# Second pass of a fused attention and gated feed-forward kernel: queue order of the x low parts, and the pace of the weight conversions

## The chip, the cores and the metric

One core of one Trainium2 chip runs the whole program. The metric is the device time of one execution in microseconds; a kernel's time is the median of its runs.

## The reference

Block-causal attention (8 batches, 8 heads, 576 tokens, head size 64, blocks of 64), followed by a feed-forward layer with a product of two branches:

```python
scores = scale * np.matmul(q, k.transpose(0, 1, 3, 2))
scores = np.where(block_i >= block_j, scores, -1000000000.0)
attn = softmax(scores)
x = (attn @ v).transpose(0, 2, 1, 3).reshape(4608, 512)
out = ((x @ w_a) * (x @ w_b)) @ w_out        # 512 -> 1536 -> 512
```

Everything is fp32 and the weights come to the chip as 64-bit floats.

## The kernel before, in words

**Products in three parts.** TensorE works on fp32r operands here. Each fp32 operand is split into a high part (a copy rounded by ScalarE) and a low part (operand minus high part, made by VectorE or GpSimd), and each product is the sum of three matmuls: high x high, high x low, low x high. So each activation that enters a product first needs a copy on ScalarE (line 110 or lines 680 to 684) and a subtraction (line 113 or lines 687 to 691).

**Stages.** The hidden dimension of 1536 is cut into 12 blocks of 128, numbered f. Up to about 690 us the attention runs together with the first pass of the feed-forward layer over f = 0 to 3 (`first_pass`). Then comes the loop at line 800, with two rounds: `ps_ = 0` works on f = 4 to 7 and `ps_ = 1` on f = 8 to 11. The text calls this loop the second pass. Each round goes over `NT2 = 6` tiles of 768 tokens. In this document tiles are counted through: tiles 0 to 5 are `ps_ = 0`, tiles 6 to 11 are `ps_ = 1`.

**A tile.** It is four units (`pair_unit`, one per f) and then `pair_out`. A unit computes seven products with a fast 2x2 scheme: y, x, w and v first, and then three more products accumulate in the banks of x, w and v. Between them VectorE adds the partial results: `u = x + u` (line 726), `t = w + u` (728), `t = v + t` (730), `c = w + u` (732), `t = c * t` (733), `u = v + u` (735), `u = x * u` (736, remembered as `last["hf"]`). Line 726 reads x's bank, and the next x product is added into that bank, so TensorE waits for line 726. The results t and u are split by ScalarE (line 110) and GpSimd (line 113) into (hb, lb) and (ha, la). `pair_out` multiplies these with the output weights: 96 matmuls on line 754, those of hb ahead of those of ha; line 813 adds the partial sums of earlier rounds, and line 814 stores them. Unit and `pair_out` together are 4 x 42 + 96 = 264 matmuls.

**Next tile's x.** `load_x` (line 660) loads raw x of the next tile on SP's queue. `sums_x` (line 669) forms the seven sums that the fast scheme needs, for two halves kp = 0 and 1: first the sums and the high parts (lines 675 to 684), then the low parts `xl` (lines 687 to 691). The low parts of kp = 0, and the first two of kp = 1, are on VectorE; the last two of kp = 1 (lines 690 and 691) are on GpSimd. `xl` has one buffer per half, so a low part can be written only when the last unit of the tile in work has read the old one. `nm` is the tile's name, `"0_1"` to `"0_6"` for what is prepared during `ps_ = 0`.

**Conversions.** `convert_w` turns 64-bit weights into fp32 high and low parts: per part five VectorE operations (lines 139, 143, 145, 147, 149), one ScalarE operation, and then sums and splits (lines 165 to 178, or line 110 with 113). It is a generator; each `next` issues one step. During `ps_ = 0` the weights of f = 8 to 11 are converted: 8 parts `wab` of six steps and then 4 parts `wo` of five steps, 68 steps in all, on operand buffers with one copy each. Finished parts go through one staging buffer `st` to HBM (`wabd`, `wod`, line 205), and are loaded from there (lines 839 and 854) when tile 5 has freed the weight buffers. `background(start + k * T2 / 2.4 / pace)` at line 827 is called at each matmul of a unit and issues steps until the count is reached; `pace` is `STEP2` from tile 1 on. At line 851, behind `pair_out` of tile 5, `background(1e4)` issues whatever is left.

**What sets the order.** The framework orders each engine's queue at compile time: an instruction that is ready earlier by its own model of time may go ahead of one that stands earlier in the program, and the engine then runs its queue strictly in order. `behind_of(ins, key)` adds an edge that waits for nothing at run time, but puts `ins` behind the instruction `last[key]` in the queue of its engine. Conversion steps have had such an edge to `last["hf"]` all along; so have two of the x sums of `"0_6"` (line 678).

Of the kernel before, what the change touches and what calls it, by code (L numbers as in the profile page):

```python
# [14 lines left out]
ALU = mybir.AluOpType  # L15
# [23 lines left out]
MORE = 6  # L39
PREF = True  # L40
STEP = 800
STEP2 = 1600
LATE = 1
LO2 = lambda nc: nc.vector
CONVP = [1]*12
# [7 lines left out]
def attention_then_bilinear_ffn(  # L53
# [10 lines left out]
    nc = tc.nc  # L64
# [40 lines left out]
    def f32(ap):  # L105
        return ap.bitcast(F32)

    def split(hi, lo, src, hi_eng, lo_eng):
        if hi_eng is nc.scalar:
            nc.scalar.copy(hi, src)  # L110
        else:
            hi_eng.tensor_copy(hi, src)
        return lo_eng.tensor_tensor(lo, src, f32(hi), op=ALU.subtract)  # L113

    last = {}

    def behind_of(ins, key):
        if key in last:
            tc.add_manual_dep(ins.ins, last[key].ins.name, NOSYNC, reason="after work that is waited for")
# [35 lines left out]
    def parts(fs):  # L155
        return [(f, i) for f in fs for i in range(KP)] + [(f, KP) for f in fs]
# [23 lines left out]
    def convert_w(todo, lo_eng, paced=False, stage=None):  # L180

        def ahead(f, i):
            return fetch(wab[f, :, i] if i < KP else wo[f], f"w{f}_{i}")

        raw = ahead(*todo[0])
        for k, (f, i) in enumerate(todo):
            now, raw = raw, ahead(*todo[k + 1]) if k + 1 < len(todo) else None
            xf, spare = yield from convert(now, f"w{f}_{i}", paced)
            if stage:
                st = stage.tile([P, 2, NW if i < KP else NO, P], F32R, tag="st", name=f"st{f}_{i}")  # L190
            if i == KP:
                if not stage and w_sb[f][1] is None:
                    new_wo(f)
                o = st.rearrange("p j c n -> p j (c n)") if stage else w_sb[f][1]
                split(o[:, 0], o[:, 1], xf, nc.scalar, lo_eng)
            elif f < F1:
                ab = w_sb[f][0]
                hi, lo = (ab[:, j, i].rearrange("p c n -> p (c n)") for j in range(2))
                split(hi, lo, xf, nc.scalar, lo_eng)
            else:  # L200
                ab = st if stage else w_sb[f][0][:, i]
                yield from sums(ab[:, 0], ab[:, 1], xf, spare, paced)
            if stage:
                f -= F1 + F2
                nc.sync.dma_start(wod[f] if i == KP else wabd[f, i], f32(st).rearrange("p j c n -> p (j c n)"))
            yield
# [18 lines left out]
    def h_tile(kind, n, dt, nm):  # L225
        return hpool.tile([P, T2], dt, tag=f"h{kind}", name=nm, bufs=(10, 6)[kind])[:, :n]
# [419 lines left out]
    def bank(nm):  # L646
        nonlocal n_bank
        n_bank += 1
        return (ps_mm if n_bank % 8 < 2 else ps_more).tile([P, 512], F32, tag="mm", name=nm)
# [19 lines left out]
    def sums_x(raw, kp, nm):  # L669

        hi = xk.tile([P, NW, T2], F32R, tag="xh", name=f"xh_{nm}_{kp}", bufs=3)
        t = tpool.tile([P, 3, T2], F32, tag="xt", name=f"xt_{nm}_{kp}")
        a, b = raw[2 * kp:2 * kp + 2]
        v = nc.vector
        for ins in (v.tensor_tensor(t[:, 1], b[:, 1], a[:, 1], op=ALU.subtract),
                    v.tensor_tensor(a[:, 1], a[:, 1], a[:, 0], op=ALU.subtract)):
            if nm == f"0_{NT2}":
                behind_of(ins, "hf")
        v.tensor_tensor(t[:, 0], b[:, 1], a[:, 1], op=ALU.subtract)
        nc.scalar.copy(hi[:, 0:2], a)  # L680
        nc.scalar.copy(hi[:, 2:4], t[:, :2])
        v.tensor_tensor(t[:, 2], b[:, 0], t[:, 0], op=ALU.subtract)
        nc.scalar.copy(hi[:, 4:6], b)
        nc.scalar.copy(hi[:, 6], t[:, 2])
        yield
        lo = xk.tile([P, NW, T2], F32R, tag="xl", name=f"xl_{nm}_{kp}", bufs=2)
        v.tensor_tensor(lo[:, 0:2], a, f32(hi[:, 0:2]), op=ALU.subtract)
        v.tensor_tensor(lo[:, 2:4], t[:, :2], f32(hi[:, 2:4]), op=ALU.subtract)
        e = nc.gpsimd if kp else v
        e.tensor_tensor(lo[:, 4:6], b, f32(hi[:, 4:6]), op=ALU.subtract)  # L690
        e.tensor_tensor(lo[:, 6], t[:, 2], f32(hi[:, 6]), op=ALU.subtract)
        yield hi, lo


# [3 lines left out]
    def pair_unit(f, xs, nm, hs, halves):  # L698

        w = w_sb[f][0]  # L700
        y, x, w_, v_ = (bank(f"ps{i}_{nm}")[:, :T2] for i in "yxwv")

        def prod(ps, what, start, kps=range(KP)):
            iw, ix = what
            for kp in kps:
                (xh, xl), wt = xs[kp], w[:, kp]
                for i, j in ((0, xh), (0, xl), (1, xh)):
                    nc.tensor.matmul(  # L708
                        ps, wt[:, i, iw], j[:, ix], start=start and kp == 0 and i == 0 and j is xh,
                        stop=kp == KP - 1 and i == 1, skip_group_check=not start)  # L710
                    yield

        if halves:
            for ps, what, kp in ((y, Y, 0), (x, X1, 0), (w_, W1, 0), (y, Y, 1), (x, X1, 1), (v_, V1, 0),
                                 (w_, W1, 1), (v_, V1, 1)):
                yield from prod(ps, what, True, [kp])
        else:
            for ps, what in ((y, Y), (x, X1), (w_, W1), (v_, V1)):
                yield from prod(ps, what, True)
        k = (f - F1) % F2  # L720
        (ha, la), (hb, lb) = (
            [h_tile(int(4 * k + 2 * j + i >= 10), T2, F32R, f"h{i}_{nm}_{j}") for i in range(2)] for j in range(2))
        u, t, c = (upool.tile([P, T2], F32, tag=f"u{i}", name=f"u{i}_{nm}", bufs=2 - i // 2) for i in range(3))
        v = nc.vector
        nc.scalar.copy(u, y)
        v.tensor_tensor(u, x, u, op=ALU.add)  # L726
        yield from prod(x, X2, False)
        v.tensor_tensor(t, w_, u, op=ALU.add)  # L728
        yield from prod(w_, W2, False)
        v.tensor_tensor(t, v_, t, op=ALU.add)  # L730
        yield from prod(v_, V2, False)
        v.tensor_tensor(c, w_, u, op=ALU.add)
        v.tensor_tensor(t, c, t, op=ALU.mult)  # L733
        split(hb, lb, t, nc.scalar, nc.gpsimd)
        v.tensor_tensor(u, v_, u, op=ALU.add)
        last["hf"] = v.tensor_tensor(u, x, u, op=ALU.mult)
        split(ha, la, u, nc.scalar, nc.gpsimd)
        hs[f] = (ha, la), (hb, lb)

    def pair_out(fs, hs, nm, out):  # L740

        todo = [(j, o) for j in (1, 0) for o in range(NO)]
        n = {}

        def run(j, o, fs_):
            k = j, o
            if k not in n:
                n[k] = 0, bank(f"pso{j}_{o}_{nm}")[:, :T2]
            i, ps = n[k]
            osl = slice(o * P, (o + 1) * P)  # L750
            for f in fs_:
                (hh, hl), wt = hs[f][j], w_sb[f][1]
                for a, b in ((0, hh), (0, hl), (1, hh)):
                    nc.tensor.matmul(ps, wt[:, a, osl], b, start=i == 0, stop=i == 3 * len(fs) - 1)  # L754
                    i += 1
            n[k] = i, ps
            if i == 3 * len(fs):
                out(j, o, ps)

        for k in todo[:2]:  # L760
            run(*k, fs[:-1])
        for k in todo[:2]:
            run(*k, fs[-1:])
        for k in todo[2:]:
            run(*k, fs)
# [14 lines left out]
    k = 0  # L780
# [8 lines left out]
    for kp in range(KP):  # L789
        g = sums_x(raw, kp, "0_0")  # L790
        next(g)
        xs.append(next(g))
# [4 lines left out]
    k = 0  # L797


    for ps_ in range(2):  # L800
        fs = list(range(F1 + ps_ * F2, F1 + (ps_ + 1) * F2))
        for tt in range(NT2):
# [18 lines left out]
            nm = f"z{ps_}_{tt}"  # L821
# [23 lines left out]
            if ps_ == 0 and tt == 0:  # L845
                background(1e4)
                conv = convert_w(parts(range(F1 + F2, NF)), nc.vector, paced=True, stage=stage)
                n_conv, start, k, pace = 0, 0, 0, STEP2
            pair_out(fs, hs, nm, out)
# [44 lines left out]
```

## Time and profile before

| what | value |
|---|---|
| median of 3 runs | 1277.81 us (1276.7 to 1278.86) |
| profiled execution | 1281.83 us |
| its span, first to last instruction | 1279.8 us |
| granted TensorE clock over the span | 0.988 |
| first product of tile 0, of tile 1 | 698.79 us, 747.01 us |
| first product of tile 6, end of the last tile's products | 993.57 us, 1276.28 us |

The profile is of one execution. It lists, for each engine, busy time and idle time with what ended the wait; the windows view gives busy times between two moments, and the timeline each instruction with its start and duration. Matmuls are pipelined, so in a full stream TensorE starts one about every 0.176 us although each lasts 0.34 us.

### The profile page before, as it was taken

The page shows a single profiled execution, that of the slowest core. Times are in us where ns is not written, and L with a number is a line of the kernel's source. Part 1 is how long each engine was busy: PE and PEld are TensorE (multiplying, and loading weights), DVE is VectorE, ACT ScalarE, POOL GpSimd, SP SyncE. Part 2 cuts the span into 40 slices and gives each one's busy share as a digit, 9 for nine tenths or more (in the row PEclk, how much of TensorE's full clock was granted, in tenths as well). Part 3 has the DMA queues.
Part 4 walks back from the last instruction along what each step waited for, and adds up shares of the span by engine and source line. Part 5 has one row for each costly group of instructions (what it writes and reads, how often), then busy time and mean ns, then how long its engine had stood idle before and what let it go on. Part 6 is the DMA issues. An engine that isn't in the chain of part 4 may idle for free.

```text
span 1279.8 us, 23524 instructions
## 1 busy us (share of the span) xinstructions
PE 1239.3 (97%) x7849; PEld 1173.2 (92%) x7849; DVE 999.2 (78%) x2389; ACT 683.6 (53%) x1722; POOL 554.9 (43%) x679
## 2 busy tenths in 40 slices
PE   9988999999999999999988998999999999999998
PEld 5668998999999999999988998999999999999998
DVE  6878887777887877877699999899967577577553
ACT  5788787788787788888745423233222222122210
POOL 4567565566665565665422322223223123123231
PEclk8999999999999999999998999999999999999999
DMA  5467766777767767676225355364466442243131
GB/s 195 132 167 201 187 174 175 178 171 181 170 167 179 179 171 176 167 178 155 87 94 171 100 180 194 139 206 164 141 220 244 145 149 79 70 149 98 52 99 62
DMA packets 93496, 196.58 MB, mean 154 GB/s; under 512 B 11968, under 2 KB 52928, under 8 KB 93376
## 3 DMA queue, kind: packets, MB, share of 16 engines
q1 hardware_dynamic: 88768, 185.64, 51.4%
q10 hardware_dynamic: 4608, 9.44, 2.0%
q8 instruction: 63, 1.03, 0.3%
q14 instruction: 57, 0.47, 0.1%
HBM read 96.47 MB, written 47.19 MB: 112 GB/s over the span
## 4 chain that ended last, share of the span: by engine, by line
PE 71%; DVE 15%; DMA 4%; issue 4%; ACT 3%; POOL 2%; SPq 1%; ACTq 0%; DVEq 0%; POOLq 0%
PE pso_z L754 13%; PE ps L217 12%; PE tp L468 7%; PE psx_z L708 6%; PE psw_z L708 6%; PE psv_z L708 6%; PE pso L217 4%; PE s L392 4%; PE psy_z L708 3%; PE av L517 3%; PE av L523 3%; PE sl L392 2%; DMA kp<-kT 2%; PE av L507 2%; DVE sw L147 1%
## 5 line engine op out<-in xcount | busy, mean ns | idle before, releaser
L113 POOL TENSOR_TENSOR h_z<-u_z,h_z 128x384 fp32r<-128x384 f32 x96 | 112.8, 1175 | 391.4 <-ACT h_z L110 379.8
L217 PE MATMUL ps<-xh,wab 128*128 128x288 f32 x1024 | 241.8, 304 | 1.2 <-ACT a L241 1.2
L754 PE MATMUL pso_z<-h_z,wo 128*128 128x384 f32 x1152 | 204.0, 335 | 4.5 <-POOL h_z L113 4.5
L445 POOL TENSOR_SCALAR e<-e,rc 128x512 f32<-128x512 f32 (+3 forms) x256 | 151.6, 604 | 127.9 <-DVE rc L442 118.1
L754 PEld LDWEIGHTS pso_z<-h_z,wo 128*128 128x128 f32 x1152 | 199.6, 188 | 7.0 <-POOL h_z L113 7.0
L217 PEld LDWEIGHTS ps<-xh,wab 128*128 128x128 f32 x1024 | 172.3, 189 | 4.7 <-ACT a L241 1.4
L472 DVE TENSOR_TENSOR al<-tp,ah 128x512 fp32r<-128x512 f32 x224 | 131.6, 608 | 31.5 <-ACT ah L470 31.0
L217 PE MATMUL ps<-xl,wab 128*128 128x288 f32 x512 | 154.1, 301 | 0.0
L468 PE MATMUL tp<-ident,e 128*128 128x128 f32 x832 | 136.1, 278 | 10.4 <-POOL e L445 4.0
L470 ACT CAST ah<-tp 128x512 fp32r<-128x512 f32 x224 | 116.4, 531 | 50.3 <-PE tp L468 47.5
L110 ACT CAST h_z<-u_z 128x384 fp32r<-128x384 f32 x96 | 49.3, 514 | 167.7 <-DVE u_z L733 160.2
L217 PE MATMUL pso<-hh,wo 128*128 128x288 f32 x512 | 128.1, 311 | 4.3 <-ACT hh L110 4.3
L708 PE MATMUL psx_z<-xh,wab 128*128 128x384 f32 x384 | 118.5, 344 | 7.2 <-DVE u_z L726 6.7
L468 PEld LDWEIGHTS tp<-ident,e 128*128 128x128 f32 x832 | 100.8, 142 | 25.7 <-POOL e L445 9.5
L401 ACT ACTIVATE e<-s,nm 128x192 f32<-128x192 f32 (+2 forms) x192 | 101.5, 529 | 32.4 <-DVE nm L398 23.2
L708 PE MATMUL psw_z<-xh,wab 128*128 128x384 f32 x384 | 117.0, 340 | 0.8 <-DVE u_z L728 0.8
L708 PE MATMUL psv_z<-xh,wab 128*128 128x384 f32 x384 | 116.7, 339 | 0.5 <-DVE u_z L730 0.4
L398 DVE TENSOR_REDUCE nm<-s 128x1 f32<-128x192 f32 (+3 forms) x256 | 109.9, 431 | 2.4
L217 PEld LDWEIGHTS ps<-xl,wab 128*128 128x128 f32 x512 | 96.5, 188 | 3.4
L217 PEld LDWEIGHTS pso<-hh,wo 128*128 128x128 f32 x512 | 88.3, 192 | 6.6 <-ACT hh L110 5.3
L113 POOL TENSOR_TENSOR v<-vr,v 128x320 fp32r<-128x320 f32 x56 | 50.2, 897 | 89.3 <-ACT v L110 67.9
L392 PE MATMUL s<-k,q 128*128 128x256 f32 x336 | 81.2, 322 | 2.2 <-ACT e_s L401 1.9
(142 smaller groups left out, 2919.5 us busy)
## 6 DMA issues: line engine op xcount, KB each, us to landing
k<-kp SPq DMA_DIRECT2D x112, 288.0 KB, 3.8
xr<-xd SPq DMA_DIRECT2D x48, 384.0 KB, 3.5
pt<-part SPq DMA_DIRECT2D x96, 192.0 KB, 3.5
q<-qp SPq DMA_DIRECT2D x112, 160.0 KB, 2.6
raww<-wab SPq DMA_DIRECT2D x24, 512.0 KB, 3.8
qp<-qT SPq DMA_DIRECT2D x32, 320.0 KB, 3.2
vr<-vm SPq DMA_DIRECT2D x64, 160.0 KB, 3.1
kp<-kT SPq DMA_DIRECT2D x32, 288.0 KB, 3.5
```

What stands on the lines that cost most here:

```text
L110: nc.scalar.copy(hi, src)
L113: return lo_eng.tensor_tensor(lo, src, f32(hi), op=ALU.subtract)
L217: mm = nc.tensor.matmul(ps, w_, d_, start=(i == 0), stop=(i == n - 1))
L392: mark = nc.tensor.matmul(ps[:, :w], qm[:, q0[t]:q0[t] + P], kk[:, :w], start=(i == 0), stop=(i == len(ks) - 1))
L398: nc.vector.tensor_reduce(nm[:, t:t + 1], view, axis=AX.X, op=ALU.max, negate=True)
L401: nc.scalar.activation(out, view, AF.Exp, bias=bias, accum_out=sm[:, t, :1])
L445: nc.gpsimd.tensor_scalar(ev, ev, rc[:, t:t + 1], 1.0, op0=ALU.mult, op1=ALU.mult)
L468: mark = nc.tensor.transpose(tp[:, c], src, ident)
L470: nc.scalar.copy(ah[:, :m, cols], tp[:, :m])
L472: return nc.vector.tensor_tensor(al[:, :m, cols], tp[:, :m], f32(ah[:, :m, cols]), op=ALU.subtract)
L708: nc.tensor.matmul(ps, wt[:, i, iw], j[:, ix], start=start and kp == 0 and i == 0 and j is xh, stop=kp == KP - 1 and i == 1, skip_group_ch ...
L754: nc.tensor.matmul(ps, wt[:, a, osl], b, start=i == 0, stop=i == 3 * len(fs) - 1)
```

## The change

Three edits. `STEP2`, the pace of the conversions from tile 1 on, goes from 1600 to 2800. The four low-part subtractions of `sums_x` get an ordering edge for the tiles prepared during `ps_ = 0`, except the very first: those on VectorE behind `last["hf"]` (line 736 of the last unit), and the two GpSimd ones of kp = 1 behind `last["la"]`. `pair_unit` remembers its last GpSimd split as `last["la"]`.

```diff
-STEP2 = 1600
+STEP2 = 2800
...
         lo = xk.tile([P, NW, T2], F32R, tag="xl", name=f"xl_{nm}_{kp}", bufs=2)
-        v.tensor_tensor(lo[:, 0:2], a, f32(hi[:, 0:2]), op=ALU.subtract)
-        v.tensor_tensor(lo[:, 2:4], t[:, :2], f32(hi[:, 2:4]), op=ALU.subtract)
         e = nc.gpsimd if kp else v
-        e.tensor_tensor(lo[:, 4:6], b, f32(hi[:, 4:6]), op=ALU.subtract)
-        e.tensor_tensor(lo[:, 6], t[:, 2], f32(hi[:, 6]), op=ALU.subtract)
+        for k, ins in enumerate((
+                v.tensor_tensor(lo[:, 0:2], a, f32(hi[:, 0:2]), op=ALU.subtract),
+                v.tensor_tensor(lo[:, 2:4], t[:, :2], f32(hi[:, 2:4]), op=ALU.subtract),
+                e.tensor_tensor(lo[:, 4:6], b, f32(hi[:, 4:6]), op=ALU.subtract),
+                e.tensor_tensor(lo[:, 6], t[:, 2], f32(hi[:, 6]), op=ALU.subtract))):
+            if nm[0] == "0" and nm != "0_0":
+                behind_of(ins, "la" if k > 1 and kp else "hf")
         yield hi, lo
...
         last["hf"] = v.tensor_tensor(u, x, u, op=ALU.mult)
-        split(ha, la, u, nc.scalar, nc.gpsimd)
+        last["la"] = split(ha, la, u, nc.scalar, nc.gpsimd)
```

## The prediction

> **What bounds the kernel now.** I read the page first, then the windows view cut at the first product of each tile, the list of what TensorE waited for, and the timelines of VectorE and GpSimd at the places found.
>
> ```profile
> span 1279.8 us, 23524 instructions
> PE 1239.3 (97%) x7849; PEld 1173.2 (92%) x7849; DVE 999.2 (78%) x2389; ACT 683.6 (53%) x1722; POOL 554.9 (43%) x679
> ```
>
> TensorE (PE) is the bound. The change touches only the loop that begins near 699 us, so what matters is how far its tiles are from an undisturbed one. The next answer has tiles 1 to 7, one to a row: length, then busy time of each engine with its count, granted clock, DMA share and GB/s.
>
> ```profile
> core 0: us, PE busy (x) PEld busy (x) DVE busy (x) ACT busy (x) POOL busy (x), PEclk, DMA share, GB/s
> 747.01:799.95 52.94, 47.58 (x265) 45.45 (x265) 48.96 (x86) 17.63 (x30) 13.58 (x10) 1.00 0.53 175
> 799.95:848.53 48.58, 47.34 (x265) 45.57 (x265) 43.69 (x76) 15.55 (x27) 13.52 (x10) 1.00 0.49 158
> 848.53:897.37 48.84, 47.26 (x266) 45.55 (x265) 46.47 (x81) 17.05 (x29) 13.49 (x10) 1.00 0.54 187
> 897.37:945.79 48.42, 47.51 (x266) 45.62 (x265) 41.65 (x64) 13.11 (x23) 13.47 (x10) 1.00 0.47 151
> 945.79:993.57 47.78, 46.73 (x266) 46.19 (x265) 32.19 (x52) 12.36 (x21) 12.49 (x10) 1.00 0.71 249
> 993.57:1043.93 50.36, 48.27 (x266) 47.78 (x265) 34.33 (x56) 12.77 (x23) 13.14 (x10) 0.97 0.44 141
> 1043.93:1090.39 46.46, 46.46 (x265) 46.29 (x265) 31.33 (x51) 11.37 (x20) 13.14 (x10) 1.00 0.34 107
> ```
>
> Tile 7 is the floor: 46.46 us, TensorE busy throughout, VectorE 31.33. Over it, tiles 1 to 5 lose 6.48 + 2.12 + 2.38 + 1.96 + 1.32 = 14.26 us and tile 6 loses 3.90. That is the most that this change can win, apart from a little in tile 0. VectorE explains where: tiles 1 to 4 hold 17.6 + 12.4 + 15.1 + 10.3 = 55.4 us more VectorE time than tile 7, which is the conversions. What TensorE waited for, in tiles 1 to 5, then from 994 us on, then around tile 0:
>
> ```profile
> PE psx_z L708 <- DVE u_z L726: 4.3, 8, 1.5
> PE pso_z L754 <- POOL h_z L113: 4.0, 3, 2.6
> PE psw_z L708 <- DVE u_z L728: 0.8, 2, 0.4
> PE psv_z L708 <- DVE u_z L730: 0.4, 1, 0.4
> ```
>
> ```profile
> PE psx_z L708 <- DVE u_z L726: 2.1, 1, 2.1
> ```
>
> ```profile
> PE pso_z L754 <- POOL h_z L113: 0.6, 1, 0.6
> PE psx_z L708 <- DVE u_z L726: 0.3, 1, 0.3
> ```
>
> Two kinds of wait, then: inside units for VectorE's sums, and at the start of `pair_out` for the last unit's split on GpSimd (POOL). The named waits of tiles 1 to 5 are 9.5 us and the tiles lose 14.26; the rest is slower restarts after each wait and weight loads that waited. So I size the sum by the tiles' lengths and use the waits only to say what belongs to which edit.
>
> **Part 1, the low parts behind the last product.** The end of tile 1, VectorE first, then POOL (start, duration, line):
>
> ```profile
> 779.84 0.55 DVE L732 TENSOR_TENSOR u_z<-psw_z,u_z 128x384 f32<-128x384 f32 x1
> 780.31 0.94 DVE L687 TENSOR_TENSOR xl<-xr,xh 128x768 fp32r<-128x768 f32 x1
> 781.17 0.55 DVE L733 TENSOR_TENSOR u_z<-u_z,u_z 128x384 f32<-128x384 f32 x1
> ...
> 782.11 0.95 DVE L688 TENSOR_TENSOR xl<-xt,xh 128x768 fp32r<-128x768 f32 x1
> 782.98 0.55 DVE L736 TENSOR_TENSOR u_z<-psx_z,u_z 128x384 f32<-128x384 f32 x1
> ...
> 788.48 1.78 DVE L688 TENSOR_TENSOR xl<-xt,xh 128x768 fp32r<-128x768 f32 x1
> ```
>
> ```profile
> 782.57 2.20 POOL L690 TENSOR_TENSOR xl<-xr,xh 128x768 fp32r<-128x768 f32 x1 [6.48 <-ACT xh L683]
> 784.71 1.73 POOL L113 TENSOR_TENSOR h_z<-u_z,h_z 128x384 fp32r<-128x384 f32 x1
> ```
>
> The edges take L687 and L688 out from between L732 and L736: L733 comes 0.87 us earlier (781.17 - 0.87 = 780.30) and L736 1.7 us. L690 on POOL, which stood ahead of the split, goes behind both splits, so the split could start near 782.6 rather than 784.71. Both gains act on the wait of 2.6 us; together they are 2.1 to 3.0, so I take it as gone. The other two waits in the 4.0 are 1.4 us together and go by the same two steps; of tile 0's 0.6 us I count all, since L733's 0.87 covers it. Nothing is added but edges. What is moved later is 4 low parts of kp = 0 and 2 of kp = 1 on VectorE, and 2 on POOL. All VectorE work in this stretch stays the same, so what is behind it (the additions of line 813, the release of raw x and with it four loads on SP) moves by under 2 us. The next tile's products start 17 us after the last unit (96 of the tile's 264 matmuls, 46.46 x 96/264), and VectorE's low parts end at 790.3 now, 11 us after L732 read that unit's products: covered, with 4 us to spare after such a move. If that cover were gone, each us late would be a us on TensorE.
>
> There is a price inside: the low part now meets the split on POOL.
>
> ```profile
> 1068.53 1.02 POOL L113 TENSOR_TENSOR h_z<-u_z,h_z 128x384 fp32r<-128x384 f32 x1 [0.33 <-POOL h_z L113]
> 1075.40 1.46 POOL L113 TENSOR_TENSOR h_z<-u_z,h_z 128x384 fp32r<-128x384 f32 x1 [5.85 <-ACT h_z L110]
> ```
>
> In tile 7 the split takes 1.02 us inside the tile, and 1.46 us at its end, where VectorE runs low parts. A low part in front of it costs at worst its own duration, 0.95 us (L688 above). The Trainium skill, SBUF — State Buffer, "Who interferes with whom", says that a VectorE instruction with two SBUF inputs and a GpSimd one that reads SBUF lock each other out, and that the second to start waits for the whole first. The 0.44 us of tile 7 agree with it; which of the two would start first behind L736 no trace here shows.
>
> **Part 2, the slower conversions.** 8 parts of six steps and 4 of five are 68 steps. A tile issues 4 x 42 = 168 calls at 160/1600 step each, 16.8 steps; at 2800 it is 9.6. So before, the steps end after four tiles; afterwards five tiles take 48 steps, which are exactly the 8 `wab` parts, and the last 20 steps, the 4 `wo` parts, come in one go at line 851. A step costs 55.4 / 68 = 0.82 us of VectorE.
>
> What a step does to TensorE is seen where a unit begins:
>
> ```profile
> 756.93 0.56 DVE L736 TENSOR_TENSOR u_z<-psx_z,u_z 128x384 f32<-128x384 f32 x1
> 757.40 1.01 DVE L139 TENSOR_SCALAR sw<-raww 128x512 int32<-128x512 int32 x1
> 758.34 0.41 DVE L143 TENSOR_SCALAR mw<-raww 128x512 int32<-128x512 int32 x1
> 758.78 1.40 DVE L145 SCALAR_TENSOR_TENSOR mw<-raww,mw 128x512 f32<-128x512 uint16 x1
> 760.10 0.55 DVE L726 TENSOR_TENSOR u_z<-psx_z,u_z 128x384 f32<-128x384 f32 x1
> ```
>
> Three steps, released by L736, are 1.01 + 0.41 + 1.40 = 2.8 us ahead of L726, for which TensorE waits. With fewer steps there are 2 or 3 instead of 4 to a unit (42 x 160/2800 = 2.4). That this brings down the loss more than in proportion I can't count on: 2 or 3 steps still fit into the same spot. So I scale: tiles 2 and 3 have no part-1 wait of size, and lose 2.12 + 2.38 = 4.5 us over 12.4 + 15.1 = 27.5 us of conversions, 0.164 us each. Five tiles with 48 x 0.82 = 39.4 us lose 6.4 us. The bounds: nothing, if two steps always fit, and 5 x 2.25 = 11.3 us, if each tile loses what tiles 2 and 3 lose now. The linear value lies between and is the only one with a row behind it.
>
> **Part 3, the 20 steps at line 851.** They are 20 x 0.82 = 16.4 us of VectorE, queued behind tile 5's last unit: part fills the 17 us of `pair_out`, the rest lies among tile 6's first units. Four `wo` parts in a row have been there before, in tile 0:
>
> ```profile
> 704.71 0.68 DVE L113 TENSOR_TENSOR wo<-xw,wo 128x512 fp32r<-128x512 f32 x1
> 718.92 0.68 DVE L113 TENSOR_TENSOR wo<-xw,wo 128x512 fp32r<-128x512 f32 x1
> ```
>
> (718.92 - 704.71) / 3 = 4.7 us a part, and TensorE waited only 0.3 us for VectorE there (row above). Here each part also passes the single staging buffer and HBM. What tile 6 loses now has another cause:
>
> ```profile
> 997.20 0.56 DVE L675 TENSOR_TENSOR xt<-xr,xr 128x384 f32<-128x384 f32 x1 [2.12 <-DMA xr<-xd]
> 999.46 0.55 DVE L726 TENSOR_TENSOR u_z<-psx_z,u_z 128x384 f32<-128x384 f32 x1
> ```
>
> VectorE stands still for a load of tile 7's x, with tile 6's L726 queued behind it; TensorE waits 2.1 us, and the clock row says 0.97, (1 - 0.97) x 50.36 = 1.5 us more. With 16 us of conversions in the same queue, this wait may be covered, or the loads come later still. At the rate above the burst alone costs 16.4 x 0.164 = 2.7 us. I take tile 6's loss as unchanged at 3.9, made up otherwise. Bounds: 1 us (the wait covered, tile 0's 0.3 and some restarts) and 16 us (rival 1). The `wo` loads of line 854 have until tile 6's `pair_out`, one tile of 46 us after tile 5's.
>
> **Sum.** 14.3 - 6.4 = 7.9 from tiles 1 to 5, 0.6 from tile 0, 0 from tile 6: 8.5 us. The profiled execution goes from 1281.8 to 1273.3. It lies 4.0 us over the median of the runs, so the median goes from 1277.8 to 1269.3.
>
> **Rivals.**
>
> 1. *Slower: the last 20 steps run in series with their DMAs.* Per part a raw load and a store:
>
> ```profile
> raww<-wo SPq DMA_DIRECT2D x12, 512.0 KB, 3.4
> wod<-st SPq DMA_DIRECT2D x4, 512.0 KB, 3.0
> ```
>
> If neither is hidden, a part takes 4.7 + 3.4 + 3.0 = 11.1 us, and four take 44 us, of which `pair_out` covers 17. The other 28 us, 2.5 parts, lie in tile 6, and in each VectorE stands 6.4 us with unit work queued behind: 16 us in place of 3.9. That gives 1269.3 + 12 = 1281. It turns the sign once tile 6 loses over 3.9 + 8.5 + 2.6 = 15 us. Against it: the next raw load is issued one part ahead, and tile 0's four parts hid theirs. For it: the one staging buffer and VectorE's 2.12 us wait for a load at this very place. Chance 0.07.
>
> 2. *The steps that hurt stay.* If each of tiles 1 to 5 goes on losing 2.25 us, 3.0 us are won there and 0.6 in tile 0, and the burst's 2.7 come on top of tile 6: about 0.9 us won, 1276.9. For it: what stands between L736 and L726 is already only three steps. Against it: tile 4 lost less with fewer conversions. Chance 0.12.
>
> 3. *Tile 6 comes free as well.* If the burst covers the load, tile 6 loses 1 us: 1266.4. Chance 0.16.
>
> 4. *The low parts lock out POOL's split.* If L687 starts first at every tile's end, the split is 0.95 us later than I have it in each of the three waits of 4.0 us, which then keep some 2.6 us: 1271.9. This is the case that the skill's rule of the lock makes possible. Chance 0.10.
>
> That the edges do nothing is excluded for L687, L688 and L690, which stand in front of what they are now to follow.
>
> **Numbers.** The forecast, 1269.3, has 0.55. From 1264.5 (rival 3, with tiles 1 to 5 losing 4.5 rather than 6.4) to 1276.0 (rival 2 with a little won in proportion) it holds 8 in 10; what is left out is rival 1 and most of rival 2. The bound of 0.2%, 2.6 us, is about what a measurement tells from no change. Faster: forecast and rivals 3 and 4, 0.81. Within 0.2%: rival 2, 0.12. Slower: rival 1, 0.07.
>
> **What the changed profile would show.** Right: L687 behind L736 at the ends of tiles 0 to 5, the split of the last unit ahead of L690, no wait of `pso_z` for POOL over 0.5 us; tiles 1 to 5 each 47 to 48.5 us with VectorE near 39 busy; `wo` parts from `pair_out` of tile 5 into tile 6's first units. Wrong: a `pso_z` wait that stays, tiles 2 to 4 at 48.5 or more, or tile 6 over 54 us.

## The result and the profile after

The changed kernel takes 1271.91 us (median of 9 runs, 1269.18 to 1276.22) against 1277.81 of before: a ratio of 0.9944, 95% interval 0.9930 to 0.9958. So it won 5.9 us where 8.5 were forecast. Its profiled execution took 1273.54 us, span 1271.6. A second measurement (e14 below) gave 0.9909 (0.9881 to 0.9936): the size of the gain is known to a few us only.

The windows view of the changed kernel, cut like that of before at the first product of each tile (tiles 1 to 7; line numbers of the unit and of what follows are 3 higher than before, and the low parts are lines 689 to 692):

```profile
core 0: us, PE busy (x) PEld busy (x) DVE busy (x) ACT busy (x) POOL busy (x), PEclk, DMA share, GB/s
745.34:792.32 46.98, 46.69 (x266) 45.79 (x266) 41.67 (x68) 13.70 (x26) 13.22 (x10) 1.00 0.44 137
792.32:839.55 47.23, 47.01 (x266) 45.87 (x265) 42.77 (x69) 14.55 (x26) 12.98 (x10) 1.00 0.47 154
839.55:887.10 47.55, 47.22 (x266) 45.98 (x266) 42.98 (x71) 15.53 (x27) 13.26 (x10) 1.00 0.48 158
887.10:934.58 47.48, 47.14 (x265) 45.96 (x265) 40.55 (x65) 12.09 (x22) 13.26 (x10) 1.00 0.44 140
934.58:983.33 48.75, 47.14 (x266) 46.18 (x265) 40.18 (x66) 13.11 (x23) 13.24 (x10) 1.00 0.78 276
983.33:1035.80 52.47, 49.48 (x265) 48.68 (x265) 46.33 (x80) 19.03 (x31) 13.77 (x10) 0.93 0.67 219
1035.80:1082.25 46.45, 46.45 (x266) 46.28 (x265) 31.33 (x51) 11.38 (x20) 13.18 (x10) 1.00 0.34 104
```

Tiles 1 to 5 now lose 0.52 + 0.77 + 1.09 + 1.02 + 2.29 = 5.69 us over the floor of 46.46, instead of 14.26. Tile 6 loses 6.01 instead of 3.90. Tile 0 is as long as before (48.33 and 48.22). That is 6.4 us won in the loop. The span shrank by 8.2; the other 1.8 us lie ahead of the loop, where nothing was changed: tile 0's first product is at 697.02 instead of 698.79. Over the 14 profiles of this study that moment lies between 694.4 and 701.8 us, so it is scatter. The tiles' lengths repeat far better (5.69 and 5.61 us for tiles 1 to 5, 6.01 and 5.53 for tile 6, in two profiles of the changed kernel), and the experiments are read by them first. One thing can spoil this: a stretch of some 3 us in which TensorE's granted clock is halved. It comes after some waits and not after others (last section), and it is most of the reason why tiles 1 to 5 lose 14.26 us in the profile of before and 16.15 in that of e9, whose program is the same up to there.

What TensorE waited for in the changed kernel, in tiles 1 to 5, then from 982 us on, then around tile 0:

```profile
PE psx_z L711 <- DVE u_z L729: 1.7, 4, 1.2
PE pso_z L757 <- POOL h_z L113: 0.4, 1, 0.4
```

```profile
PE psx_z L711 <- DVE u_z L729: 1.7, 1, 1.7
PE psw_z L711 <- DVE u_z L731: 1.3, 1, 1.3
```

```profile
PE pso_z L757 <- POOL h_z L113: 0.8, 1, 0.8
PE psx_z L711 <- DVE u_z L729: 0.2, 1, 0.2
```

The waits of `pair_out` for GpSimd fell from 4.0 to 0.4 us, and those for VectorE from 5.5 to 1.7. The end of tile 1 shows the new order, VectorE and then GpSimd:

```profile
775.42 0.56 DVE L736 TENSOR_TENSOR u_z<-u_z,u_z 128x384 f32<-128x384 f32 x1
775.90 0.55 DVE L738 TENSOR_TENSOR u_z<-psv_z,u_z 128x384 f32<-128x384 f32 x1
776.48 0.56 DVE L739 TENSOR_TENSOR u_z<-psx_z,u_z 128x384 f32<-128x384 f32 x1
776.96 1.62 DVE L689 TENSOR_TENSOR xl<-xr,xh 128x768 fp32r<-128x768 f32 x1
```

```profile
776.73 2.73 POOL L113 TENSOR_TENSOR h_z<-u_z,h_z 128x384 fp32r<-128x384 f32 x2 [5.36 <-PE psv_z L711]
779.43 2.58 POOL L691 TENSOR_TENSOR xl<-xr,xh 128x768 fp32r<-128x768 f32 x1
```

The low part (L689) is behind the last product (L739), and both splits go ahead of the low part on GpSimd. In tile 6 something else shows:

```profile
988.14 0.55 DVE L676 TENSOR_TENSOR xr<-xr 128x384 f32<-128x384 f32 x1
988.61 0.68 DVE L149 TENSOR_TENSOR xw<-mw,sw 128x512 f32<-128x512 f32 x1
989.21 0.55 DVE L729 TENSOR_TENSOR u_z<-psx_z,u_z 128x384 f32<-128x384 f32 x1
991.10 0.43 DVE L139 TENSOR_SCALAR sw<-raww 128x512 int32<-128x512 int32 x1 [1.34 <-DMA raww<-wo]
```

The leftover conversions stand in VectorE's queue around tile 6's first sums: L729 comes late, and behind it L139 of the next `wo` part waits 1.34 us for its raw weights while L731, for which TensorE waits, is queued behind it. The two waits of TensorE in tile 6 are 1.7 + 1.3 = 3.0 us. The granted clock of tile 6, 0.93, stands for (1 - 0.93) x 52.47 = 3.7 us by estimate; together this is more than the 6.0 us that the tile loses, so the two overlap in part.

### The profile page after: what moved, and what is told of

Its sections match the earlier page's. It is cut to its first block, busy times and chain, and to the rows that moved or that the text cites. A ratio compares the mean times of both kernels' runs of the same rounds, so it can differ in the third digit from the quotient of the medians.

```text
span 1271.6 us, 23516 instructions
## 1 busy us (share of the span) xinstructions
PE 1235.8 (97%) x7849; PEld 1172.4 (92%) x7849; DVE 1006.1 (79%) x2389; ACT 683.3 (54%) x1722; POOL 556.9 (44%) x679
## 4 chain that ended last, share of the span: by engine, by line
PE 74%; DVE 14%; issue 3%; DMA 3%; ACT 3%; POOL 2%; SPq 0%; ACTq 0%; DVEq 0%; POOLq 0%
PE pso_z L757 14%; PE ps L217 12%; PE tp L468 7%; PE psx_z L711 7%; PE psw_z L711 6%; PE pso L217 5%; PE psv_z L711 5%; PE s L392 4%; PE av L517 3%; PE psy_z L711 3%; PE av L523 3%; PE sl L392 2%; DMA kp<-kT 2%; DVE sw L147 1%; DVE nm L398 1%
## 5 line engine op out<-in xcount | busy, mean ns | idle before, releaser
L468 PE MATMUL tp<-ident,e 128*128 128x128 f32 x832 | 135.8, 278 | 11.1 <-POOL e L445 4.0
```

The costliest lines, as they stand in the source:

```text
L468: mark = nc.tensor.transpose(tp[:, c], src, ident)
```

## The experiments

My theory at this point: the edges removed the waits for GpSimd, the pace the waits for VectorE, and the 20 steps issued in one go at the end of tile 5 (the burst) are what tile 6 loses. The rivals: the pace does all, or the edges do all, or tile 6 loses by the loads of tile 7's x as it did before. The table has, for each, what tiles 1 to 5 and tile 6 lose over 46.46 us a tile in its profile, and the ratio to the kernel before. Each ratio is against runs of the kernel before on the same chip: one chip for e1 to e4, a second for e5 to e10, a third for e11 to e13 and the changed kernel's second measurement (e14). "x7" means that the sums of tile 7's x (lines 675 and 676 of `"1_1"`) are put behind the products of tile 6 as well.

| kernel | edges | STEP2 | x7 | tiles 1 to 5 | tile 6 | both | ratio (95%) |
|---|---|---|---|---|---|---|---|
| before | no | 1600 | no | 14.26 | 3.90 | 18.2 | 1 |
| changed | yes | 2800 | no | 5.69 | 6.01 | 11.7 | 0.9944 (0.9930 to 0.9958) |
| changed, again | yes | 2800 | no | 5.61 | 5.53 | 11.1 | 0.9909 (0.9881 to 0.9936) |
| e1 | yes | 1600 | no | 11.95 | 8.21 | 20.2 | 0.9994 (0.9982 to 1.0006) |
| e2 | no | 2800 | no | 9.59 | 0.61 | 10.2 | 0.9936 (0.9921 to 0.9951) |
| e3 | yes | 1970 | no | 8.46 | 4.65 | 13.1 | 0.9954 (0.9939 to 0.9968) |
| e4 | yes | 2800 | yes | 5.52 | 6.14 | 11.7 | 0.9938 (0.9917 to 0.9959) |
| e5 | yes | 1970 | yes | 8.73 | 1.44 | 10.2 | 0.9939 (0.9920 to 0.9959) |
| e8 | yes | 1600 | yes | 12.20 | 1.35 | 13.6 | 0.9952 (0.9933 to 0.9970) |
| e9 | no | 1600 | yes | 16.15 | 1.33 | 17.5 | 0.9986 (0.9969 to 1.0003) |
| e10 | no | 1970 | yes | 13.20 | 1.36 | 14.6 | 0.9978 (0.9962 to 0.9994) |
| e11 | yes, drain early | 2800 | yes | 5.63 | 5.10 | 10.7 | 0.9920 (0.9894 to 0.9947) |
| e12 | yes | 2350 | yes | 6.85 | 3.33 | 10.2 | 0.9922 (0.9893 to 0.9951) |
| e13 | yes, drain early | 2350 | yes | 6.84 | 3.49 | 10.3 | 0.9928 (0.9908 to 0.9948) |

**The edges alone (e1).**

```diff
 # the changed kernel, but
-STEP2 = 2800
+STEP2 = 1600
```

> The edges alone, with the pace of before (STEP2 = 1600). If the edges remove the waits of pair_out for GpSimd and nothing else, tiles 1 to 5 lose 14.3 - 4 to 5 = 9 to 10 us, tile 6 stays at 3.9 lost, and the median lies 4 to 5 us under before, near 1273. If the slower pace does all of it (rival), this kernel is within 1 us of before. If the edges do all of it, it is at 1272 like the changed kernel. Tile 6 tells the price of the burst: 3.9 here against 6.0 in the changed kernel if the 20 steps at the end of tile 5 made the difference.

The time did not move: 0.9994. First the waits of TensorE in tiles 1 to 6, then tiles 1, 5 and 6 in the windows view, then VectorE at the start of tile 6:

```profile
PE psx_z L711 <- DVE u_z L729: 10.7, 8, 5.8
PE psw_z L711 <- DVE u_z L731: 0.8, 2, 0.4
PE psv_z L711 <- DVE u_z L733: 0.4, 1, 0.4
```

```profile
745.05:796.90 51.85, 48.87 (x265) 47.40 (x265) 46.39 (x83) 16.83 (x30) 13.89 (x10) 0.97 0.52 172
942.86:989.30 46.44, 46.44 (x266) 46.21 (x265) 32.41 (x52) 11.68 (x20) 12.56 (x10) 1.00 0.70 240
989.30:1043.96 54.66, 48.86 (x265) 48.39 (x265) 35.34 (x59) 13.45 (x23) 13.18 (x10) 0.94 0.44 141
```

```profile
990.77 1.01 DVE L816 TENSOR_TENSOR pt<-pso_z,pt 128x384 f32<-128x384 f32 x2
996.64 0.56 DVE L675 TENSOR_TENSOR xt<-xr,xr 128x384 f32<-128x384 f32 x1 [4.86 <-DMA xr<-xd]
...
998.89 0.55 DVE L729 TENSOR_TENSOR u_z<-psx_z,u_z 128x384 f32<-128x384 f32 x1
```

The edges did what they say: there is no wait for GpSimd left in tiles 1 to 6, and tile 5 is at the floor (46.44). Yet tiles 1 to 5 won only 2.3 us: in tile 1 TensorE waited 2.0 us at the start of a unit (1.5 us at that place before), with a lower clock behind it, (1 - 0.97) x 51.85 = 1.6 us. And tile 6 gave back 4.3: VectorE stood 4.86 us at a load of tile 7's x, with tile 6's L729 behind it, and TensorE waited 5.8 us. It is the wait of before, 2.1 us there, made longer. My forecast for the edges, about 4 us, fell; the rival that the pace does all fits this run.

**The pace alone (e2).**

```diff
 # the kernel before, but
-STEP2 = 1600
+STEP2 = 2800
```

> The slower pace alone (STEP2 = 2800), no edges on the low parts. If the two edits act on different waits, this one keeps the waits of pair_out for GpSimd where the last unit's chain is late (in tile 1 it may be on time, since less is queued there): tiles 1 to 5 lose 5.7 (as in the changed kernel) plus up to 4, tile 6 loses 6 (the burst is there as well): 0.5 to 4 us slower than the changed kernel, 1272.5 to 1276. If the edges do nothing, it equals the changed kernel at 1272.

As fast as the changed kernel, 0.9936. Waits in tiles 1 to 6, and tiles 5 and 6:

```profile
PE psx_z L708 <- DVE u_z L726: 2.4, 7, 1.3
PE pso_z L754 <- POOL h_z L113: 2.0, 1, 2.0
PE psw_z L708 <- DVE u_z L728: 0.2, 1, 0.2
```

```profile
935.41:987.48 52.07, 48.73 (x266) 47.54 (x266) 41.25 (x70) 14.60 (x26) 12.61 (x10) 0.97 0.79 275
987.48:1034.54 47.06, 46.71 (x265) 45.88 (x265) 44.11 (x75) 17.54 (x30) 13.39 (x10) 1.00 0.66 217
```

The slower pace by itself removes tile 1's wait for GpSimd. The only long one left is tile 5's, 2.0 us with a lower clock behind it. Tile 6 has the same 20 steps as in the changed kernel, and loses 0.61 us. So the burst alone is not what tile 6 loses. Tiles 5 and 6 together lose 6.2 us here and 8.3 in the changed kernel: the time that tile 5 no longer waits for GpSimd comes back in tile 6. VectorE's first sum of tile 6 in e2:

```profile
990.39 0.56 DVE L726 TENSOR_TENSOR u_z<-psx_z,u_z 128x384 f32<-128x384 f32 x1
```

In the changed kernel it is at 989.21 (L729 above), 1.2 us earlier, though TensorE begins tile 6 there 4.15 us earlier, at 983.33 instead of 987.48. So most of what TensorE won in tile 5 it spends in tile 6 on waiting for VectorE. The rest is clock: without what the lower clock cost by the rows, (1 - 0.97) x 52.07 = 1.6 us here and 3.7 in the changed kernel, tiles 5 and 6 lose 4.6 us in both, by this estimate.

**No burst (e3), and tile 7's sums moved (e4, e5).**

```diff
 # e3: the changed kernel, but
-STEP2 = 2800
+STEP2 = 1970
 # e4: the changed kernel, but
-            if nm == f"0_{NT2}":
+            if nm in (f"0_{NT2}", "1_1"):
                 behind_of(ins, "hf")
 # e5: both
```

> Edges, and a pace of 1970, at which the 68 steps end with tile 5's last unit, so that nothing is left to issue in one go. If the burst is what tile 6 loses, tile 6 comes back to 3.9 (the load that VectorE waits for is still there) and tiles 1 to 5 lose in proportion to 13.6 instead of 9.6 steps, 5.7 x 1.4 = 8 us: about as fast as the changed kernel, 1271 to 1273. If the loss of a step grows faster than in proportion, tiles 1 to 5 lose 10 or more: 1274. If tile 6's loss has nothing to do with the burst, tile 6 stays at 6.

> The changed kernel, and the first two sums of tile 7's x also behind the last product of the unit before them (as is done for tile 6's already), so that no work for tile 7 stands in VectorE's queue among tile 6's first units. If part of tile 6's 6.0 us comes from that work (two sums of 0.5 us and what they wait for), tile 6 loses 4.5 to 5 and the median is 1 to 1.5 us under the changed kernel. If the loss is all of the conversions and their loads, it is unchanged at 1272.

> Edges, pace 1970 (no burst), and the sums of tile 7's x behind tile 6's products. In the run with 1970 and without that last step, tile 6 lost 4.65 us, most of it in one wait of 3.1 us of x's products for VectorE, which stood at a load of tile 7's x. If that is the cause, tile 6 falls to 1 us or less and the ratio to before goes from 0.9954 to about 0.9925, some 9 to 10 us under before. If the wait just moves to other work, the ratio stays near 0.995.

e3 came out at 1274.35 us, 0.9954, slower than the 1271 to 1273 that I had expected: tiles 1 to 5 lose 8.46, close to proportion (5.7 x 13.6/9.6 = 8.1), and tile 6 4.65, with one wait of 3.1 us for the load of tile 7's x. In e4 tile 6 did not get better (6.14): with the burst there, the conversions and their loads are the cause. In e5 tile 6 falls to 1.44. So tile 6 has two causes, and each hides the other: without a burst it is the load of tile 7's x ahead of tile 6's sums, with it the burst. The ratio of e5, 0.9939, fell by less than I had expected (0.9925); the loss in the profile fell as expected.

**What the edges are worth with tile 6 undisturbed (e8, e9, e10).**

```diff
 # e8: the changed kernel with x7 and STEP2 = 1600
 # e9: the kernel before with x7
 # e10: the kernel before with x7 and STEP2 = 1970
-            if nm == f"0_{NT2}":
+            if nm in (f"0_{NT2}", "1_1"):
```

> Edges at the pace of before, and the sums of tile 7's x behind tile 6's products. Theory: the edges do win 2.3 us in tiles 1 to 5 (14.3 to 12.0 lost in the run with the edges alone) and it is given back at tile 6, which lost 8.2 there. Then without the wait for tile 7's load this kernel is 7 us under the edges alone: ratio to before about 0.994. Rival: the edges are worth nothing wherever tile 7's sums stand, and this one is no faster than the kernel before with the same step.

> The kernel before with one step alone: the sums of tile 7's x behind tile 6's products. If tile 6's 3.9 us of before are that wait for a load (2.1 us) and the lower clock behind it (1.5 us), this wins 3 to 3.5 us, a ratio of 0.997 to 0.9975. If it is no cause, ratio 1.000. Beside the run with edges and this step it gives the price of the edges with tile 6 undisturbed: 2 us in their favour by the profile.

> Pace 1970 and the sums of tile 7's x behind tile 6's products, without the edges on the low parts. If the edges are worth something at this pace (no wait of pair_out for GpSimd was left with them), this loses 1 to 4 us against the same kernel with edges, at waits of pair_out for GpSimd at the ends of tiles 1 and 5. If they are worth nothing, both are equal.

Tile 6 loses 1.3 to 1.4 us in all three. At the pace of before the edges then win 17.5 - 13.6 = 3.9 us (e9 to e8), 0.9986 to 0.9952, with intervals that only just meet; at 1970 they win 14.6 - 10.2 = 4.4 us (e10 to e5), 0.9978 to 0.9939, and these two intervals do not overlap. Both comparisons are of like with like in the clock: it is 0.97 in tile 1 of e9 and of e8 (rows below, in this order), and e10 and e5 have no such stretch. The profile of before has none in tile 1, and against it the edges would seem to win only 14.26 - 12.20 = 2.1 us in tiles 1 to 5.

```profile
741.81:796.43 54.62, 49.39 (x266) 47.26 (x265) 49.27 (x86) 17.63 (x30) 13.54 (x10) 0.97 0.52 174
743.02:795.25 52.23, 48.92 (x266) 47.14 (x265) 47.36 (x83) 16.90 (x30) 13.60 (x10) 0.97 0.51 173
```

In e9 the waits for GpSimd in tiles 1 to 5 stand as they were; in e8 there are none:

```profile
PE pso_z L754 <- POOL h_z L113: 4.0, 3, 2.6
```

So the rival that the edges are worth nothing falls too: they win some 4 us, which the load of tile 7's x takes back in e1.

**When the burst is issued (e11, e12, e13).**

```diff
 # e11: the changed kernel with x7; e13: the same with STEP2 = 2350
+            if ps_ == 0 and tt == NT2 - 1:
+                background(1e4)
             pair_out(fs, hs, nm, out)
             if ps_ == 0 and tt == NT2 - 1:
-                background(1e4)
 # e12: the changed kernel with x7 and STEP2 = 2350
```

> The changed kernel with tile 7's sums behind tile 6's products, and the 20 leftover steps issued ahead of tile 5's pair_out instead of behind it, so that they stand in VectorE's queue among the low parts and pair_out's additions. If tile 6's 6 us come from the burst standing ahead of tile 6's first sums, then with most of the burst under pair_out tile 6 loses 1.5 to 3 us, and the sum of tiles 0 to 6 is 3 to 4.5 us under the changed kernel's 338.8. If the loss is that of the loads and stores of the wo parts in series (0.6 to 1.3 us of waits each), it stays at 5 to 6.

> Edges, tile 7's sums behind tile 6's products, pace 2350: 57 of the 68 steps in tiles 1 to 5, 11 left for the burst (two wo parts). By proportion tiles 1 to 5 lose between 5.5 (2800) and 8.7 us (1970), about 7, and tile 6 between 6.1 and 1.4, about 3.5: a sum of 10.5, between or equal to its neighbours (11.7 and 10.2). If the price of the burst only begins when it is longer than pair_out's free VectorE time, tile 6 stays near 1.4 and the sum is 8.5.

> The same at pace 2350 with the leftover steps ahead of pair_out: two wo parts fit under pair_out, so tile 6 loses 1.4 us as with no burst, tiles 1 to 5 about 7: the sum of tiles 0 to 6 at 334 to 335, the best of all, 9 to 10 us under before. If a step ahead of pair_out delays the low parts and with them tile 6's first products, tile 6 loses more than without.

> The changed kernel again, on the chip of the three above, to compare with them: 0.9944 of before, within the interval of 0.993 to 0.996; tiles 1 to 5 lose 5.7 us and tile 6 6.0, since the order of each queue is fixed.

Issuing the leftover steps earlier did not help: tile 6 still loses 5.10 us in e11. From 960 us on, TensorE waited there for something new:

```profile
PE psw_z L711 <- DVE pt L816: 1.2, 1, 1.2
PE psy_z L711 <- DVE pt L816: 1.1, 1, 1.1
```

L816 is the addition that empties a bank of `pair_out`; the steps stood ahead of it, and tile 6's first unit needed the bank. With 11 steps left over (e12) tile 6 loses 3.33, between 1.44 for none and 6.14 for 20, about 0.2 us a step; issuing them early changes nothing (3.49 in e13, where I had expected 1.4). Tiles 1 to 5 go the other way, 8.7, 6.9, 5.5 us for 1970, 2350 and 2800. So the sums of e5, e11, e12 and e13, and that of e2, are within 0.6 us of each other and 0.4 to 1.5 us under the changed kernel's two profiles (11.7 and 11.1). In the times no version beats the changed kernel measurably: on one chip, e11, e12 and e13 had 0.9920 to 0.9928 and the changed kernel 0.9909, with intervals that overlap. The changed kernel's second measurement repeated the losses of its tiles (5.61 and 5.53 us), but its ratio is under the 0.993 to 0.996 that I had expected; its interval overlaps that of the first.

## Why the prediction was right, and where it was not

**Right: tiles 1 to 5.** Forecast to lose 6.4 us, they lose 5.7. But two errors nearly cancel in that, and so far the closeness is luck. VectorE's time for the 48 steps was put at 39.4 us; the rows above give 41.67 + 42.77 + 42.98 + 40.55 + 40.18 less 5 x 31.33, which is 51.5 (some 2 us of it are the burst's first steps). The price of 0.82 us was an average over all 68 steps, while the 48 are all of the longer `wab` kind (a `wo` part's five steps are 3.6 us of VectorE operations where the changed kernel runs them, 0.72 us a step), and the operations also lasted longer than before (line 149 in these tiles: 1.09 us on average instead of 0.81; why is not shown). And the loss per us of it was put at 0.164 and is 5.7/51.5 = 0.11. Spreading the steps helps more than in proportion, which I had not dared to count on. By the runs with the edges this lies between 1600 and 1970: a step costs 12.0/68 = 0.18 us at 1600, part of it the lower clock in tile 1, and 0.13, 0.12 and 0.12 at 1970, 2350 and 2800.

**Right in what they remove, not in what they add: the edges.** I put down to the edges the 4.0 us of waits for GpSimd. They do remove them (e1). The pace alone removes tile 1's 2.6 us and leaves one wait of 2.0 us, in tile 5 (e2). At this pace the edges take tiles 1 to 5 from 9.59 to 5.69 us, but tile 6 from 0.61 to 6.01: no gain of the edges is left to measure, 0.9936 without them and 0.9944 and 0.9909 with them. In tiles 1 to 5 the gains of the two edits do add (2.3 us by the edges alone, 4.7 by the pace alone, 8.6 together); over the loop they don't, since tile 6 takes back what the edges win.

**Wrong: tile 0.** The step "of tile 0's 0.6 us I count all" failed: the wait is 0.8. VectorE, GpSimd and ScalarE at that place, each in its own timeline:

```profile
729.98 0.95 DVE L689 TENSOR_TENSOR xl<-xr,xh 128x768 fp32r<-128x768 f32 x1
```

```profile
730.07 3.43 POOL L113 TENSOR_TENSOR h_z<-u_z,h_z 128x384 fp32r<-128x384 f32 x2 [3.82 <-ACT h_z L110]
```

```profile
728.75 0.83 ACT L681 CAST xh<-xt 128x768 fp32r<-128x768 f32 x1
729.49 0.51 ACT L110 CAST h_z<-u_z 128x384 fp32r<-128x384 f32 x1
```

The copy on ScalarE still came behind L681, so the split gained nothing at its start, and the low part L689 started 0.09 us ahead of it: the two splits take 3.43 us here and 2.73 in tile 1, where the split started first and L689 took 1.62 instead of 0.95 us. That is rival 4, at one tile's end of six; at the other five the split started first. The time of tile 0 as a whole can't show this, since it differs by more between two profiles of the changed kernel (48.33 and 47.20 us). The trace agrees here with what the Trainium skill says of the lock (SBUF — State Buffer, "Who interferes with whom"): the one that starts second waits.

**Mis-sized: tile 6.** "I take tile 6's loss as unchanged at 3.9, made up otherwise" was the failing term: it is 6.0, inside the bounds of 1 to 16. The wait for tile 7's load did give way to the burst, as I had it, and the 2.7 us for the burst were too few: the two waits are 3.0 us, and the lower clock costs 3.7 us instead of the 1.5 of before. Rival 1's mechanism is there in a small form (VectorE's 1.34 us at a raw load). That the edges would lengthen tile 6's wait, which e1 shows, I did not see: with tile 5 at the floor, tile 6 starts sooner while tile 7's loads, which stand between `pair_out`'s stores in SP's queue, do not keep up: the last of the four was issued 0.6 us ahead of tile 6's first product before (992.93 and 993.57), and 0.9 us behind it in e1 (990.24 and 989.30).

**Sum.** 8.6 (tiles 1 to 5) - 0.1 (tile 0) - 2.1 (tile 6) = 6.4 us in the loop, 5.9 in the medians, against 8.5. Rival 2 (tiles 1 to 5 lose as before) and rival 3 (tile 6 comes free) did not come about; tile 6 comes near rival 3's 1 us in e5, with no burst and tile 7's sums moved, and in e2, where tile 5 is late. The median is, to 0.1 us, the 1271.9 of rival 4, and that is chance: of the waits that this rival keeps, 2.6 us, tiles 1 to 5 have 0.4 left, and the 2.6 us that are missing from the forecast lie mostly in tile 6. Of the signs named, tile 5's 48.75 us and VectorE's 40 to 43 us a tile lie a little outside what was said.

What stays open: that tile 6 loses 0.6 us in e2 and 6.0 in the changed kernel with the same burst is put down to its later start in e2, by the timelines of two profiles; no run sets this apart from the other differences of the two queues. No run had the edges without those for tile 6's x.

## What to carry to other kernels

Where an engine runs a queue in order, a wait that is removed comes back at the next place where work for later stands ahead of work that is due: look for the next load in the queue before counting a gain. Gains that add in the tiles where two edits act need not add over the loop, so run each alone and both together. Count a loop's gain by the lengths of its own tiles, when the rest of the program scatters by more than the gain, and look whether a stretch of lower clock lies in one profile and not in the other.

## What the runs showed of the hardware

A wait of TensorE of some 2 us or more was sometimes followed by about ten matmuls at half the rate (0.32 us apart instead of 0.176), and sometimes not. Behind the 2.0 us wait in tile 1 of e1:

```profile
752.58 0.52 PE L711 MATMUL psx_z<-xh,wab 128*128 128x384 f32 x1
752.90 0.52 PE L711 MATMUL psw_z<-xh,wab 128*128 128x384 f32 x1
753.22 0.52 PE L711 MATMUL psw_z<-xl,wab 128*128 128x384 f32 x1
```

The same wait at the end of tile 1, from the timeline and with the granted clock of the 10 us around it from the windows view (the column behind POOL's); the kernel before first, then e9:

```profile
786.49 0.79 PE L754 MATMUL pso_z<-h_z,wo 128*128 128x384 f32 x3 [2.58 <-POOL h_z L113]
```

```profile
780.00:790.00 10.00, 7.42 (x43) 7.10 (x42) 10.00 (x10) 4.59 (x8) 6.87 (x4) 1.00 0.48 127
```

```profile
781.38 0.79 PE L754 MATMUL pso_z<-h_z,wo 128*128 128x384 f32 x3 [2.57 <-POOL h_z L113]
```

```profile
775.00:785.00 10.00, 7.43 (x35) 7.11 (x35) 10.00 (x10) 4.49 (x8) 6.86 (x4) 0.86 0.47 130
```

The first wait cost its 2.6 us, the second (1 - 0.86) x 10 = 1.4 us more. That is most of the difference between tile 1's 52.95 us in the one profile and 54.62 in the other. Of the 11 waits of 2.0 us and more in the loop of the 14 profiles that stand by themselves, 7 were followed by the half rate; the shortest of these were 2.0 us, in e1, e2 and e8. The Trainium skill (TensorE: Matmul & The Clock Gate, Part 1) tells of a free-running window of 3.4 us after which an idle TensorE falls to half its clock. A free-running window fits "sometimes"; that 2 us of waiting are enough is not what it says, and here the traces decide.
